# Moving two operands of one matrix product to other byte places in on-chip memory

## The chip, the cores and the metric

The kernel runs on one core of one Trainium2 chip. The metric is device time in microseconds (us) from the first to the last instruction of one execution. Three runs of the kernel before took 2555.57, 2558.36 and 2559.72 us; the median is 2558.36 us.

## What is computed

The reference is a spectral filter followed by a two-layer network, in single precision:

```
X  = rfft(x, axis=1)                       # x: 8 batches x 3008 positions x 256
Yr = X.real @ w_r - X.imag @ w_i + b_r     # the projection: 256 x 256 complex weights
Yi = X.real @ w_i + X.imag @ w_r + b_i
Yr, Yi = soft_threshold(Yr, 0.01), soft_threshold(Yi, 0.01)
y  = irfft(Yr + 1j * Yi, n=3008, axis=1)   # 24064 tokens x 256
h  = y @ w_in                              # first product:  256 -> 2048
g  = maximum(0.01 * h, h)
out = g @ w_out                            # second product: 2048 -> 256
```

## The kernel before

The length 3008 is split as 47 x 64, so the transforms are matrix products too. Each of the 8 batches passes three stages that go through DRAM: `fwd(b)` (sums of 47, constants `fa0` and `fa1`), `mid(b)` (sums of 64, projection, threshold, inverse sums of 64) and, for the tokens, `inverse` (the last sums of 47). Batches 0 and 1 of `fwd` and batch 0 of `mid` run ahead of the main loop in plain single precision. The main loop `moe()` takes tokens in 47 chunks of 512 and the 2048 hidden features in 8 steps `q` of 256 a chunk. A step issues the first product (`moe_a` and `moe_b`, a Strassen scheme of seven 256-column block products) and the second product (`moe_o`, 512 columns). Between the steps a `Stream` pulls a little of `fwd(b + 1)` and `mid(b)` of the next batch. The order on every engine is settled when the program is built; TensorE takes its matmuls strictly as they stand.

Wherever single precision is needed at the faster matmul rate, a value is held as two halves, high and low (type `F32R`), and a product is three matmuls: high x high, and the two mixed ones. A matmul has a *stationary* operand, which a weight load (LDWEIGHTS, row `PEld`) puts into the array, 128 columns wide, and a *moving* operand, which streams through it, 256 or 512 columns wide. Two helpers issue them: `products` (line 80) for everything but the network's first product, `block` (line 94) for that one.

The part that the change touches is `mid(b)` for batches 1 to 7, 12 steps `j` each:

- `stage_b(j)` multiplies by `fb` (line 358) and splits the result into the halves `eh` and `el`, slices of one tile `e2` of 128 x 2 x 2 x 3 x 128 values: ScalarE writes `eh` (lines 370, 373), VectorE `el` (lines 372, 374).
- `proj(j)` is the projection: three weights (`wr`, `wn`, `wd`) x two halves of the feature axis x three terms = 18 matmuls of 256 columns. The stationary operand is a 128-column slice of `e2`, the moving one a 256-column slice of a weight. In the profile these are line 80, `psf<-wr_hi,eh` and its like; `eh` stands there for the whole tile `e2`.

`pair` lays out the constants' halves: it asks for a tile with some spare room and uses it from element `skip` on, so that `skip` sets the byte place of the operand. `split_consts` calls it for the projection's weights (names that begin with w) and for the constants of the transforms.

The places where operands begin in the built program before, in bytes modulo 128 of a partition's address; every slice of an operand is a multiple of 128 bytes further on and so begins at the same place:

| matmuls | columns | count | moving | stationary |
|---|---|---|---|---|
| first product, line 94 (`yh`, `yl` x `win`) | 256 | 7728 | 64 | 0 |
| second product, line 622 (`gh`, `gl` x `wout`) | 512 | 4512 | 64 | 64 |
| projection, line 80 (`wr`, `wn`, `wd` x `eh`) | 256 | 1512 | 96 | 64 |
| inverse sums of 64, line 80 (`zh` x `gb`) | 512 | 252 | 64 | 64 |
| sums of 47, line 80 (`xz` x `fa`) | 512, 256 | 252 | 64 | 64 |

(The first chunk's 96 first products have 512 columns, at the same places as the others.)

Of the kernel before, what the change touches and what calls it, by code (L numbers as in the profile page):

```python
# [9 lines left out]
F32R = mybir.dt.float32r  # L10
# [10 lines left out]
P = 128  # L21
# [9 lines left out]
def spectral_mlp_kernel(  # L31
# [21 lines left out]
    NH = D // P  # L53
# [12 lines left out]
    sb = ctx.enter_context(tc.tile_pool(name="sb", bufs=2))  # L66
# [4 lines left out]
    def bank(tag, bufs):  # L71
        return ps.tile([P, 512], F32, name=tag, tag=tag, bufs=bufs)
# [29 lines left out]
    def pair(name, shape, skip, spare=0):  # L102

        n = 1
        for s in shape[1:]:
            n *= s
        room = -(-n // 32) * 32 + 32
        tiles = [
            const.tile([shape[0], room + k], F32R, name=f"{name}_{p}")[:, skip:skip + n]
            for p, k in (("hi", 0), ("lo", spare))  # L110
        ]
        if len(shape) == 4:
            tiles = [t.rearrange("p (a b c) -> p a b c", a=shape[1], b=shape[2]) for t in tiles]
        elif len(shape) == 3:
            tiles = [t.rearrange("p (a b) -> p a b", a=shape[1]) for t in tiles]
        consts[name] = tuple(tiles)
        return consts[name]

    def load_plain(name, src, shape):
        consts[name] = const.tile(shape, F32, name=name)  # L120
        sync.dma_start(consts[name], src)

    def split_consts():
        for name in ("wr", "wd", "wn", "gb", "fa0", "fa1"):
            w = consts[name + "32"][0]
            hi, lo = pair(name, list(w.shape), 16 if name[0] == "w" else 8, 32 if name == "gb" else 0)
            act.copy(hi, w)
            dve.tensor_sub(lo, w, hi.bitcast(F32))

# [197 lines left out]
    def mid(b):  # L327
# [21 lines left out]
        def stage_b(j):  # L349

            u = u_t.pop(j)
            pb = bank("psh", 4) if b < 1 else bank("psf", 2)
            pv = pb.rearrange("p (a c i k) -> p a c i k", a=NH, c=2, i=2)
            for i in range(2):
                k = 2 * j + i
                for dh in range(NH):
                    s = slice(dh * P, (dh + 1) * P)
                    nc.tensor.matmul(pv[:, dh, :, i, :], u[:, i, s], fbt[:, 0:k + 2:k + 1, :], start=True, stop=True)  # L358
            pv = pb.rearrange("p (a c m) -> p a c m", a=NH, c=2)
            if b == 0:  # L360
                ef = e0[:, j % 2]
                act.copy(ef[:, :, 0:2, :], pv)
                dve.tensor_add(ef[:, :, 2, :], ef[:, :, 0, :], ef[:, :, 1, :])
                e_t[j] = (ef,)
                return
            e2 = sb.tile([P, 2, NH, 3, P], F32R, name="eh", tag="e", bufs=1)
            eh, el = e2[:, 0], e2[:, 1]
            xi = sb.tile([P, NH, P], F32, name="xi", tag="xi", bufs=1)
            act.copy(xi, pv[:, :, 1, :])
            act.copy(eh[:, :, 0:2, :], pv)  # L370
            dve.tensor_add(xi, pv[:, :, 0, :], xi)
            dve.tensor_sub(el[:, :, 0:2, :], pv, eh[:, :, 0:2, :].bitcast(F32))
            act.copy(eh[:, :, 2, :], xi)
            dve.tensor_sub(el[:, :, 2, :], xi, eh[:, :, 2, :].bitcast(F32))
            e_t[j] = (eh, el)
# [62 lines left out]
        if b:  # L438
            for s in range(NPAIR):
                if s + 2 < NPAIR:  # L440
                    load(s + 2)
                with tc.issue_after(mlp[0].ins):
                    stage_b(s)
                yield 16 * P
                yield None
                yield from proj(s)
            stage_g(NPAIR - 1)
            yield 3 * CS
            return
        for s in range(NPAIR + 3):  # L450
            if s + 2 < NPAIR:
                load(s + 2)
            if s < NPAIR:
                stage_b(s)
                yield 16 * P
            if 0 <= s - 1 < NPAIR:
                yield from proj(s - 1)
            if 0 <= s - 3 < NPAIR:
                stage_g(s - 3)
                yield 3 * CS  # L460
# [246 lines left out]
    f0.to(0.01)  # L707
    load_win(0, (sync, act))
    load_plain("fb", fb, [P, NK1 + 1, N2])
    load_weights()  # L710
    sign = const.tile([P, NK1 + NPAIR], F32, name="sign")
# [10 lines left out]
    with tc.issue_after(turned[0].ins):  # L722
        split_consts()
# [8 lines left out]
    with tc.issue_after(reads[3].ins):  # L732
        load_plain("ga", ga, [PA, 2, P])
# [152 lines left out]
```

## Time and profile before

| | |
|---|---|
| median of three runs | 2558.36 us |
| the profiled execution | 2558.46 us, of which the span from first to last instruction is 2556.7 us |
| TensorE matmul (PE) | 2515.7 us busy, 98% of the span |
| weight loads (PEld) | 2259.0 us, 88% |
| VectorE (DVE) | 1881.0 us, 74% |
| ScalarE (ACT) | 1673.5 us, 65% |
| mean granted TensorE clock | 0.995 of full |

Matmuls are pipelined: the profile gives each a duration of 280 ns or so for 256 columns, but the next one starts long before it ends. What a matmul costs a busy TensorE is the distance from its start to the next start. The chain of work that ended last counts in this way (a piece of "x6" is six matmuls, and its time runs to the next piece), and so do the start times of the timeline.

### The profile page before, as it was taken

To read this page: it belongs to the slowest core of one execution; us is meant where nothing else is said; L and a number is where in the kernel's file an instruction comes from. 1 tells how busy PE (TensorE), PEld (TensorE's weight loads), DVE (VectorE), ACT (ScalarE), POOL (GpSimd) and SP (SyncE) were. 2 spreads that over 40 slices of the span, in tenths; PEclk is the share of its full clock that TensorE was granted. 3 is DMA by queue.
4 is the path that set the end of the run, shared out by engine and by line. 5 is a ranking of instruction groups with operands and counts; after the bars stand their busy time and mean duration, and the time that the engine had idled before them with its cause. 6 is when DMAs were issued, how large, how long until landed. Compare 5 with 4: busy or idle time off the path is not lost.

```text
span 2556.7 us, 42449 instructions
## 1 busy us (share of the span) xinstructions
PE 2515.7 (98%) x16204; PEld 2259.0 (88%) x16204; DVE 1881.0 (74%) x3460; ACT 1673.5 (65%) x3151; POOL 119.3 (5%) x96
## 2 busy tenths in 40 slices
PE   6999999999999999999999999999999999999999
PEld 4689888999899998999989999899998998999998
DVE  7787777777877778777787777876768777666675
ACT  4776666677666776667756676566665676656564
POOL 0001000000000000000000000000000000000000
PEclk8999999999999999999999999999999999999999
DMA  8631133111321113211142111411114111101000
GB/s 262 184 93 49 44 88 91 42 46 49 102 70 42 50 41 109 61 51 50 38 113 58 50 45 42 113 57 50 46 38 123 55 51 44 46 17 33 9 17 17
DMA packets 119904, 165.12 MB, mean 65 GB/s; under 512 B 13597, under 2 KB 69909, under 8 KB 119701
## 3 DMA queue, kind: packets, MB, share of 16 engines
q1 hardware_dynamic: 79112, 115.54, 14.9%
q10 hardware_dynamic: 40589, 46.87, 7.1%
q8 instruction: 128, 2.10, 0.3%
q14 instruction: 75, 0.61, 0.1%
HBM read 86.60 MB, written 75.76 MB: 64 GB/s over the span
## 4 chain that ended last, share of the span: by engine, by line
PE 90%; DMA 4%; DVE 3%; ACT 2%; issue 1%; SPq 1%; ACTq 0%; DVEq 0%
PE pso L622 38%; PE psh L94 34%; PE psf L80 11%; PE psf L495 3%; PE psf L358 3%; DMA xin<-x_dram 1%; PE psh L80 1%; DMA u<-u_dram 1%; DVE gl L575 1%; DMA u_dram<-xin 1%; DVE xz L270 0%; DMA v_dram<-v 0%; DVE gf L606 0%; ACT zf L413 0%; DMA vin<-v_dram 0%
## 5 line engine op out<-in xcount | busy, mean ns | idle before, releaser
L94 PE MATMUL psh<-yh,win_hi 128*128 128x256 f32 (+1 forms) x2608 | 737.2, 284 | 2.4 <-DVE gf L606 2.4
L94 PE MATMUL psh<-yl,win_hi 128*128 128x256 f32 (+1 forms) x2608 | 727.0, 279 | 0.0
L94 PE MATMUL psh<-yh,win_lo 128*128 128x256 f32 (+1 forms) x2608 | 726.5, 280 | 0.0
L575 DVE TENSOR_TENSOR gl<-gf,gh 128x1024 fp32r<-128x1024 f32 x376 | 461.1, 1226 | 309.7 <-ACT gh L573 300.5
L622 PE MATMUL pso<-gh,wout_hi 128*128 128x512 f32 x1504 | 592.3, 394 | 1.1 <-ACT gh L573 1.1
L622 PE MATMUL pso<-gh,wout_lo 128*128 128x512 f32 x1504 | 590.4, 393 | 0.0
L622 PE MATMUL pso<-gl,wout_hi 128*128 128x512 f32 x1504 | 588.7, 391 | 1.1 <-DVE gl L575 1.1
L94 PEld LDWEIGHTS psh<-yh,win_hi 128*128 128x128 f32 x2608 | 489.3, 188 | 19.9 <-DVE gf L606 4.9
L94 PEld LDWEIGHTS psh<-yl,win_hi 128*128 128x128 f32 x2608 | 490.5, 188 | 15.6 <-issue 0.5
L94 PEld LDWEIGHTS psh<-yh,win_lo 128*128 128x128 f32 x2608 | 489.1, 188 | 2.0
L573 ACT CAST gh<-gf 128x1024 fp32r<-128x1024 f32 x376 | 395.4, 1052 | 45.1 <-PE pso L622 35.3
L609 ACT ACTIVATE gf<-gf 128x768 f32<-128x768 f32 x368 | 311.8, 847 | 158.7 <-DVE gf L606 147.6
L622 PEld LDWEIGHTS pso<-gl,wout_hi 128*128 128x128 f32 x1504 | 282.6, 188 | 61.9 <-DVE gl L575 3.0
L622 PEld LDWEIGHTS pso<-gh,wout_hi 128*128 128x128 f32 x1504 | 282.7, 188 | 48.4 <-ACT gh L573 1.9
L622 PEld LDWEIGHTS pso<-gh,wout_lo 128*128 128x128 f32 x1504 | 282.6, 188 | 45.4 <-issue 0.2
L608 ACT ACTIVATE gf<-psh 128x256 f32<-128x256 f32 x368 | 141.6, 385 | 229.8 <-PE psh L94 223.4
L606 DVE TENSOR_TENSOR gf<-psh,u 128x512 f32<-128x512 f32 x368 | 252.7, 687 | 27.7 <-PE psh L94 25.3
L590 ACT COPY p<-psh 128x256 f32<-128x256 f32 x368 | 136.7, 371 | 153.3 <-PE psh L94 144.7
L395 POOL TENSOR_TENSOR kb<-bias,kc 128x512 f32<-128x512 f32 x84 | 116.7, 1389 | 2068.3 <-ACT kc L393 1865.4
L591 DVE TENSOR_TENSOR u<-psh,p 128x256 f32<-128x256 f32 x368 | 154.8, 421 | 71.8 <-ACT p L590 70.8
L593 DVE TENSOR_TENSOR gf<-psh,u 128x256 f32<-128x256 f32 x368 | 155.1, 422 | 30.4 <-PE psh L94 16.4
L594 DVE TENSOR_TENSOR gf<-psh,gf 128x256 f32<-128x256 f32 x368 | 154.8, 421 | 5.5
(128 smaller groups left out, 3179.4 us busy)
## 6 DMA issues: line engine op xcount, KB each, us to landing
u<-u_dram SPq DMA_DIRECT2D x192, 128.0 KB, 2.8
v_dram<-v ACTq DMA_DIRECT2D x192, 128.0 KB, 2.4
out_dram<-ob SPq DMA_DIRECT2D x94, 256.0 KB, 2.0
vin<-v_dram SPq DMA_DIRECT2D x96, 240.0 KB, 3.6
xin<-x_dram SPq DMA_DIRECT2D x90, 240.0 KB, 3.1
u_dram<-xin ACTq DMA_DIRECT2D x72, 240.0 KB, 2.4
u_dram<-xin SPq DMA_DIRECT2D x24, 240.0 KB, 4.3
raw<-w_out_dram SPq DMA_DIRECT2D x8, 512.0 KB, 4.9
```

The source lines that it names most:

```text
L80: last = nc.tensor.matmul(dst, a, b, start=(i == 0), stop=(i == len(terms) - 1))
L94: mlp[:] = [nc.tensor.matmul(dst, a, b, start=start and i == 0, stop=i == 2, skip_group_check=True)]
L573: cp = act.copy(gh, g)
L575: parted[:] = [cp, dve.tensor_sub(gl, g, gh.bitcast(F32))]
L590: act.copy(p1, b1[:, lo])
L591: dve.tensor_add(u2, b1[:, hi], p1)
L593: dve.tensor_add(g[:, 3], b2[:, hi], u2)
L594: dve.tensor_add(g[:, 3], b2[:, lo], g[:, 3])
L606: dve.tensor_add(g[:, 1:3], b2.rearrange("p (k n) -> p k n", k=2), u2.unsqueeze(1).broadcast_to([P, 2, HT]))
L608: act.activation(g[:, 0], b1[:, lo], AF.Prelu, alpha=SLOPE)
L609: act.activation(g[:, 1:4], g[:, 1:4], AF.Prelu, alpha=SLOPE)
L622: mlp[:] = [nc.tensor.matmul(po, a[:, f, s], r[:, i], start=(f == 0 and j == 0), stop=(f == NF - 1 and j == 2),)]
```

## The change

Two operands get other places. `split_consts` uses `skip` 8 in place of 16 for the projection's weights, 32 bytes earlier in tiles that stay where they were: they begin at 64 in place of 96 modulo 128. The tile `e2` comes from a new helper, `placed`, that asks for 32 more values a partition and gives out the part from value 16 on: it begins 64 bytes later, at 0 in place of 64 modulo 128. The projection then has the first product's places, moving 64 and stationary 0.

The tile `e2` is 6272 in place of 6144 bytes a partition, so every ring that lies behind it moves up by 128 bytes and keeps its place modulo 128: among them `z` (`zh`), `zf`, `u`, `v`, `wout_lo`, `kb`, `t`, `y`, `odd`, `p1` and `u2`. `win`, `yh`, `yl`, `wout_hi`, `gh` and `gl` stay where they were. No instruction is added, removed or moved: on every engine the same operations stand in the same order with the same waits, and only line numbers differ (9 more behind `placed`).

```diff
+    def placed(shape, name, tag, bufs):
+
+        n = 1
+        for k in shape[1:]:
+            n *= k
+        t = sb.tile([P, n + 32], F32R, name=name, tag=tag, bufs=bufs)[:shape[0], 16:16 + n]
+        axes = " ".join("abcd"[:len(shape) - 1])
+        return t.rearrange(f"p ({axes}) -> p {axes}", **dict(zip("abcd", shape[1:])))
+
...
     def split_consts():
         for name in ("wr", "wd", "wn", "gb", "fa0", "fa1"):
             w = consts[name + "32"][0]
-            hi, lo = pair(name, list(w.shape), 16 if name[0] == "w" else 8, 32 if name == "gb" else 0)
+            hi, lo = pair(name, list(w.shape), 8 if name[0] == "w" else 8, 32 if name == "gb" else 0)
...
-            e2 = sb.tile([P, 2, NH, 3, P], F32R, name="eh", tag="e", bufs=1)
+            e2 = placed([P, 2, NH, 3, P], "eh", "e", 1)
             eh, el = e2[:, 0], e2[:, 1]
```

## The prediction

> **What bounds the kernel now.** I read the page's engine totals first, then its chain by line, then the busy time by stage, and last the chain in order of time inside the stage that the change touches. The totals and the chain:
>
> ```profile
> PE 2515.7 (98%) x16204; PEld 2259.0 (88%) x16204; DVE 1881.0 (74%) x3460; ACT 1673.5 (65%) x3151; POOL 119.3 (5%) x96
> ...
> PE 90%; DMA 4%; DVE 3%; ACT 2%; issue 1%; SPq 1%; ACTq 0%; DVEq 0%
> PE pso L622 38%; PE psh L94 34%; PE psf L80 11%; PE psf L495 3%; PE psf L358 3%; DMA xin<-x_dram 1%; PE psh L80 1%; DMA u<-u_dram 1%; DVE gl L575 1%; DMA u_dram<-xin 1%; DVE xz L270 0%; DMA v_dram<-v 0%; DVE gf L606 0%; ACT zf L413 0%; DMA vin<-v_dram 0%
> ```
>
> TensorE has work in 98% of the span, and nine tenths of the chain that ended last run through its matmuls. The projection is part of "psf L80", 11% of the chain together with the inverse sums and the sums of 47. The three stages (start, main loop with `fwd` and `mid` between, main loop alone):
>
> ```profile
> 0.00:180.00 180.00, 151.24 (x640) 108.97 (x641) 137.79 (x237) 112.41 (x207) 2.05 (x7) 0.93 0.62 184
> 180.00:2190.00 2010.00, 2002.25 (x13233) 1822.84 (x13232) 1504.93 (x2803) 1347.51 (x2585) 117.23 (x89) 1.00 0.22 61
> 2190.00:2557.00 367.00, 362.21 (x2335) 327.17 (x2333) 238.24 (x421) 213.57 (x360) 0.00 (x0) 1.00 0.07 24
> ```
>
> The columns are the stretch, its length, then the busy time of PE, PEld, DVE, ACT and POOL. Between 180 and 2190 us PE is idle for 2010.00 - 2002.25 = 7.75 us, 0.4%. So a nanosecond less between two matmuls there is very nearly a nanosecond less of the whole, and nothing else sets the pace: DVE has 2010 - 1505 = 505 us to spare. All matmuls that the change touches lie in that stretch or within 5 us of its start, as the first and last starts of the projection's groups say:
>
> ```profile
> L80 PE MATMUL psf<-wr_hi,eh x336: 277/282/385, 175.5 to 2186.0; 128*128 128x256 f32 x168
> L80 PE MATMUL psf<-wn_hi,eh x336: 278/280/288, 175.7 to 2189.5; 128*128 128x256 f32 x168
> L80 PE MATMUL psf<-wd_hi,eh x336: 277/281/363, 176.4 to 2190.2; 128*128 128x256 f32 x168
> L80 PE MATMUL psf<-wr_lo,eh x168: 277/281/286, 175.6 to 2185.9; 128*128 128x256 f32 x168
> L80 PE MATMUL psf<-wn_lo,eh x168: 277/281/286, 175.8 to 2189.3; 128*128 128x256 f32 x168
> L80 PE MATMUL psf<-wd_lo,eh x168: 277/281/365, 176.6 to 2190.0; 128*128 128x256 f32 x168
> ```
>
> That is 3 x 336 + 3 x 168 = 1512 matmuls of 256 columns, 84 steps of 18. Their durations (median 281 ns) say nothing of their cost, since the next one starts long before; nor do those of the first product, which are as long:
>
> ```profile
> L94 PE MATMUL psh<-yl,win_hi 128*128 128x256 f32 x2576 | 714.4, 278 | 0.0
> L94 PE MATMUL psh<-yh,win_lo 128*128 128x256 f32 x2576 | 713.9, 278 | 0.0
> ```
>
> What a matmul costs is read from the chain in order of time, in a stretch without waits, where each piece ends as the next begins (start, us, what):
>
> ```profile
> 1686.74 2.75 PE pso L622 x12
> 1689.49 1.42 PE psf L80 x12
> 1690.90 2.43 PE psh L94 x21
> 1693.33 0.73 PE psf L80 x6
> 1694.06 2.76 PE pso L622 x12
> ```
>
> One whole step of the projection stands here: the x12 and the x6 of line 80 are its 18 matmuls. They take 1.42 + 0.73 = 2.15 us, 119.4 ns each. The first product's 21 between them, of the same width, in the same three-term scheme and with one weight load each, take 2.43 us, 115.7 ns each. Twenty microseconds on, a step is cut into smaller pieces:
>
> ```profile
> 1709.46 0.70 PE psh L94 x6
> 1710.16 0.72 PE psf L80 x6
> 1710.89 1.72 PE psh L94 x15
> 1712.60 0.72 PE psf L80 x6
> 1713.33 2.76 PE pso L622 x12
> ```
>
> Six of the first product take 116.7 ns each, six of the projection 120.0 ns, on both sides of fifteen of the first product at 114.7 ns. And late in the kernel, where no projection is left, a run of the first product goes at 2.40 / 21 = 114.3 ns:
>
> ```profile
> 2418.34 2.40 PE psh L94 x21
> 2420.74 2.74 PE pso L622 x12
> ```
>
> So the projection's matmuls are slower than the first product's in every piece where the two can be compared, by 3.3 to 5.3 ns. What differs between them by the program is the places (96 and 64 modulo 128 against 64 and 0), the PSUM bank they write and what stands before them; the shape, the term order and the one load for each matmul are alike.
>
> **The change part by part.** *The projection's two places.* After it the projection and the first product have the same two places, so I price the 1512 matmuls by the first product's rows. The trace doesn't hold a projection at these places; its price is bounded below by 114.3 ns (the long undisturbed run) and above by the present 119.4 ns. I take 115.7 ns, the run that stands right between two pieces of the projection, which is nearest in place and surroundings; a run of six alone would give 116.7. Gain: 1512 x (119.4 - 115.7) = 5.6 us. Of it 2002.25 / 2010.00 = 99.6% lies on a busy PE, which leaves 5.6; I take 5.5, since the shorter TensorE work now and then only meets a wait that was covered. The waits that could take it back are those of PE and its weight loads on VectorE and ScalarE, for which the groups show a few us in all:
>
> ```profile
> L94 PEld LDWEIGHTS psh<-yh,win_hi 128*128 128x128 f32 x2608 | 489.3, 188 | 19.9 <-DVE gf L606 4.9 <-issue 0.2 <-ACT yh L520 0.2
> L622 PE MATMUL pso<-gl,wout_hi 128*128 128x512 f32 x1504 | 588.7, 391 | 1.1 <-DVE gl L575 1.1
> ```
>
> With `gf` (line 606) and `gl` (line 575) late by 4.9 and 1.1 us over the whole kernel, they are next if PE gets ahead, but a step that is 0.07 us shorter out of some 24 us (2010 / 84) shortens what covers them by 0.3%.
>
> *The writes into the moved operands.* ScalarE and VectorE now write `eh` from place 0 in place of 64 (four instructions a step, lines 370 to 374), and the three weights once from 64 in place of 96. Writes of one shape, 128x512, to place 0 (`win`) and to place 64 (`zh`) stand in the trace:
>
> ```profile
> L421 DVE TENSOR_TENSOR zh<-zf,zh 128x512 fp32r<-128x512 f32 x84 | 57.7, 686 | 13.8 <-ACT zh L420 13.1
> L420 ACT CAST zh<-zf 128x512 fp32r<-128x512 f32 x84 | 51.9, 618 | 1.2
> L187 DVE TENSOR_TENSOR win_lo<-cva,win_hi 128x512 fp32r<-128x512 f32 x4 | 2.8, 688 | 1.3 <-ACT win_hi L186 1.3
> L186 ACT CAST win_hi<-cva 128x512 fp32r<-128x512 f32 x4 | 2.5, 619 | 8.4 <-DVE t L405 4.8 <-DVE cva L177 3.6
> ```
>
> 686 against 688 ns and 618 against 619 ns: 84 x 4 x 2 ns = 0.7 us at most, on two engines that have hundreds to spare. Cost zero; without that cover 0.7 us.
>
> *The rings that move by 128 bytes.* They keep their place modulo 128. If only that counts they cost nothing. If 256 counted, the second product's `wout_lo` would change class; the first product tells: its `win_hi` and `win_lo` start 128 bytes apart modulo 256 (at 128 and 0), and their rows above are 278 ns both. I take zero, and keep a loss as a rival.
>
> *The order, the DMA queues and SP.* No instruction moves on any engine, so no queue is passed and no wait added: zero.
>
> Sum, against the profiled execution's own 2558.46 us (span 2556.7 us and 1.8 us around it; it is within 0.1 us of the median 2558.36 us): 2558.46 - 5.5 = 2553.0 us, 0.21% less. A measurement of this kernel can tell about 0.2%, some 5.1 us, from no change, so the forecast lies just at that edge.
>
> **The rivals.** *The place is not the cause.* The 3 to 5 ns could come from what surrounds the projection: short pieces, and another class of matmul before each. The trace speaks partly for it: the first product's own price goes from 114.3 ns in a run of 21 to 116.7 ns in a run of six and to 115.7 ns behind a projection. Against it, like pieces still differ (six at 120.0 beside six at 116.7). Then nothing happens: 2558.5 us. [...]
>
> *More than the rows of its neighbours.* If a switch between places also slows the first product behind a projection (2.43 against 2.40 us for 21), about 0.03 us come back at each of one or two such switches a step: 84 to 168 x 0.03 = 2.5 to 5 us more. With the projection at 114.3 ns itself (1512 x 5.1 = 7.7 us) the end is 2558.46 - 7.7 - 2.5 = 2548.3 us. The undisturbed rows speak for it, but few are so clean.
>
> *Slower: `wout_lo` pays.* The second product's stationary `wout_lo` goes from 64 to 192 modulo 256. If the place modulo 256 decides the price there, and by as much as the best and worst places of 256 columns differ now (5.1 ns), 1504 matmuls lose 7.7 us:
>
> ```profile
> L622 PE MATMUL pso<-gh,wout_lo 128*128 128x512 f32 x1504 | 590.4, 393 | 0.0
> ```
>
> With the projection's gain that is 2558.46 - 5.5 + 7.7 = 2560.7 us, without it 2566.2 us. It ends slower than before from 5.5 us / 1504 = 3.7 ns a matmul on. Against it stands the equality of `win_hi` and `win_lo`.
>
> *The change does not do what it says.* The built program's places are those stated, so this has no chance of its own.
>
> **How the numbers follow.** The place is the cause and the projection goes at about the first product's price: 0.62, of which 0.44 come out over 5.1 us and 0.18 under. The larger gain with the switches is the upper tail of this and included. The place is not the cause: 0.27, all within 0.2%, but for 0.02 that some other effect of the move makes it faster. The `wout_lo` loss, or a like one on a moved ring: 0.11, of which 0.08 slower by over 0.2% and 0.03 within. Faster 0.46, same 0.46, slower 0.08. The predicted time is the likeliest case's, 2553.0 us, with a range of its own of 2549 to 2556. The range for 8 in 10 takes in no effect and the spread of the runs shown (1.4 us above the median), 2560.0, and below the larger gain, 2548.5.
>
> **What would show it.** In the profile after, a step of the projection (x12 and x6 of line 80 in the chain) should take 18 x 115.7 = 2.08 us in place of 2.15, and a run of six 0.70 in place of 0.72; the first product's and the second product's pieces should stay at 2.40 and 2.74. If the projection's pieces stay at 0.72 and 1.42, the place was not the cause. If pieces of the first product behind a projection fall to 2.40, the switch was. If "pso L622 x12" grows past 2.78, a moved ring has taken it back. The prediction is wrong beyond its range if the pair 64 and 0 has a price in the projection that no row of the first product shows.

## The result and the profile after

The changed kernel is slower: median 2563.51 us of 19 runs (2560.57 to 2567.85) against 2558.36 us of 19 runs of the kernel before (2554.06 to 2564.43). The ratio is 1.002, with a 95% interval of 1.0013 to 1.0027: 3 to 7 us lost where 5.5 us were forecast to be won, and beyond the range of 2548.5 to 2560.0.

The projection did get faster. The chain in order of time of the changed kernel, at the two places that were shown of the kernel before (start, us, what; line 631 is the second product's old line 622):

```profile
1691.30 1.41 PE psf L80 x12
1692.72 2.40 PE psh L94 x21
1695.12 0.70 PE psf L80 x6
1695.82 2.79 PE pso L631 x12
...
1711.31 0.72 PE psh L94 x6
1712.03 0.71 PE psf L80 x6
1712.74 1.72 PE psh L94 x15
1714.46 0.70 PE psf L80 x6
1715.16 2.79 PE pso L631 x12
```

A step of the projection, x12 and x6 of line 80, takes 1.41 + 0.70 = 2.11 us, where it took 2.15. The first product's 21 behind the projection take 2.40 where they took 2.43. But the second product's 12 take 2.79 where they took 2.75 and 2.76. The same stands late in the kernel, where there is no projection any more:

```profile
2418.93 2.40 PE psh L94 x21
2421.33 2.78 PE pso L631 x12
```

Before, that piece took 2.74. So what the second product loses does not come from a projection beside it, and the kernel has 4512 / 12 = 376 such pieces' worth of it. The groups say it too, with durations of 395 in place of 391 and 393 ns:

```profile
L631 PE MATMUL pso<-gl,wout_hi 128*128 128x512 f32 x1504 | 593.4, 395 | 1.1 <-DVE gl L584 1.1
L631 PE MATMUL pso<-gh,wout_lo 128*128 128x512 f32 x1504 | 593.5, 395 | 0.0
```

No wait has grown: behind the second bar stands the idle time ahead of them, 1.1 and 0.0 us as before, and in the main stretch TensorE is busy for the same share of the time, 2002.36 of 2010 us where it was 2002.25, with fewer matmuls done in it (13191 where it was 13233):

```profile
180.00:2190.00 2010.00, 2002.36 (x13191) 1817.76 (x13190) 1502.11 (x2796) 1347.01 (x2579) 115.61 (x88) 1.00 0.22 61
```

For the whole kernel I took the distance from each matmul's start to the next one's, by class, leaving out those that hold a wait (over 145 ns for 256 columns, over 270 ns for 512). Each class keeps at least 98% of its matmuls. Means in ns:

| | first product, 256 columns | projection, 256 | second product, 512 |
|---|---|---|---|
| before | 115.2 | 119.5 | 229.6 |
| after | 115.2 | 117.3 | 231.8 |
| difference x count | 0 | -2.2 x 1512 = -3.3 us | +2.3 x 4512 = +10.2 us |

Together +6.9 us; the span of the profiled executions went from 2556.7 to 2563.4 us, +6.7 us. By class that is the whole account. The first product's 0 hides two shifts, though: its 1541 matmuls in runs right behind a projection went from 115.7 to 114.7 ns (-1.4 us), and most of the others, behind the second product and other classes, from 115.0 to 115.3 ns (+1.9 us).

### The profile page after: what moved, and what is told of

The parts are those of the page before. It is cut to its first block, busy times and chain, and to the rows that moved or that the text cites. A ratio compares the mean times of both kernels' runs of the same rounds, so it can differ in the third digit from the quotient of the medians.

```text
span 2563.4 us, 42449 instructions
## 1 busy us (share of the span) xinstructions
PE 2522.5 (98%) x16204; PEld 2258.9 (88%) x16204; DVE 1882.9 (73%) x3460; ACT 1676.7 (65%) x3151; POOL 119.0 (5%) x96
## 4 chain that ended last, share of the span: by engine, by line
PE 90%; DMA 4%; DVE 2%; ACT 2%; issue 1%; SPq 0%; ACTq 0%; DVEq 0%
PE pso L631 38%; PE psh L94 34%; PE psf L80 11%; PE psf L504 3%; PE psf L367 3%; DMA xin<-x_dram 2%; PE psh L80 1%; DMA u_dram<-xin 1%; DMA u<-u_dram 1%; DVE gl L584 1%; DMA v_dram<-v 0%; DVE xz L279 0%; DVE gf L615 0%; ACT gh L582 0%; ACT zf L422 0%
```

## The experiments

In all twelve kernels the operations on every engine, their order and their waits are those of the kernel before; only places differ. Theory A: a ring that moved by 128 bytes slows the second product, by its place modulo 256. Rival B: the projection's new places disturb what follows it.

**The shift alone.** The kernel before, with the tile longer and the operands where they were:

```diff
-            e2 = sb.tile([P, 2, NH, 3, P], F32R, name="eh", tag="e", bufs=1)
+            e2 = sb.tile([P, 2 * NH * 3 * P + 32], F32R, name="eh", tag="e", bufs=1)[:, :2 * NH * 3 * P].rearrange(
+                "p (a b c d) -> p a b c d", a=2, b=NH, c=3)
```

> Edit to the kernel before: the tile of the projection's operand is 128 bytes longer at its end, and both operands of the projection stay where they were (96 and 64). So every ring behind it moves up by 128 bytes as in the changed kernel, and nothing else differs. Theory A (a moved ring slows the second product): its pieces of 12 take 2.78 us as in the changed kernel, against 2.74 before; the projection stays at 1.42 and 0.73; 4512 x 2.3 ns = 10 us on top, 2568 us. Rival B (the projection's new places slow what follows it): pieces stay at 2.74 and the time at 2558 us.

Measured: 2569.96 us, ratio 1.0049 (1.0036 to 1.0061). The chain of this kernel, in the stage of the projection (line 623 is the second product):

```profile
1692.34 2.78 PE pso L623 x12
1695.11 1.42 PE psf L80 x12
1696.53 2.43 PE psh L94 x21
1698.96 0.72 PE psf L80 x6
```

The projection is as slow as ever and the second product as slow as in the changed kernel (231.9 ns). Theory A holds, B falls: 128 bytes of unused room behind one tile cost 9 to 16 us.

**The places alone.** The changed kernel, with the rings behind moved by 256 in place of 128 bytes:

```diff
-        t = sb.tile([P, n + 32], F32R, name=name, tag=tag, bufs=bufs)[:shape[0], 16:16 + n]
+        t = sb.tile([P, n + 64], F32R, name=name, tag=tag, bufs=bufs)[:shape[0], 16:16 + n]
```

> Edit to the changed kernel: the helper asks for 64 more values, not 32, so that the rings behind the tile lie 256 bytes above their old places, not 128; the projection has its new places. Theory A with place modulo 256 as what counts: the second product is back at 2.74 a piece of 12, the projection keeps 1.41 and 0.70, and the time is 3 us under the kernel before, 2555 us. If any move of the rings hurts (not modulo 256): 2.78 and 2563 us or more. Rival B: 2.78 and 2563.5 us.

Measured: 2551.68 us, ratio 0.9977 (0.9968 to 0.9986). Its chain:

```profile
1706.05 0.70 PE psf L80 x6
1706.75 1.71 PE psh L94 x15
1708.45 0.70 PE psf L80 x6
1709.16 2.74 PE pso L631 x12
```

Both are fast. So what the change set out to do is worth some 6 us (the kernel before took 2557.91 us in the runs beside it), more than the 3 us expected from the projection's own matmuls: by the distances, the projection gives 3.4 us, the first product 0.27 ns x 7728 = 2.1 us (in the runs right behind a projection it goes from 115.7 to 114.6 ns) and the second product 0.35 ns x 4512 = 1.6 us.

**Which ring.** Two kernels on the changed one; in both the tile of `wout_lo` is 128 bytes longer, so the rings behind it are 256 bytes up. In the first `wout_lo` begins 128 bytes into it, in the second at its start:

```diff
-            sb.tile([P, NF, D], F32R, name=f"wout_{p}", tag=f"wout_{p}", bufs=1) for p in ("hi", "lo"))
+            sb.tile([P, NF * D + (32 if p == "lo" else 0)], F32R, name=f"wout_{p}", tag=f"wout_{p}", bufs=1)[
+                :, 32 if p == "lo" else 0:][:, :NF * D].rearrange("p (a b) -> p a b", a=NF) for p in ("hi", "lo"))
```

(the second kernel has 0 in place of the 32 that stands behind the comma.)

> Edit to the changed kernel: wout_lo alone begins 128 bytes later in a tile that is 128 bytes longer, so it lies at 64 modulo 256 again; z, zf and u stay 128 bytes up, the rings behind wout_lo (t, v, y, odd, p1, u2) are 256 up. A1 (the second product's own operand): pieces of 12 back at 2.74, about 2555 us. A2 (z, zf or u): still 2.78, 2563.5 us. A3 (the rings behind wout_lo, read and written by ScalarE and VectorE): 2.74 and 2555 us as A1; the next run parts these two.

> As the run before (the longer tile, rings behind wout_lo 256 bytes up), but wout_lo begins at the tile's start and stays at 192 modulo 256. A1: 2.78 a piece and 2563.5 us, as the changed kernel. A3: 2.74 and 2555 us.

Measured: 2552.63 us, ratio 0.9985 (0.9975 to 0.9994), with `wout_lo` back at 64 modulo 256, and 2565.07 us, ratio 1.0031 (1.0019 to 1.0042), with it at 192. The first kernel's chain and then the second's (line 632 is the second product in both):

```profile
1687.12 0.70 PE psf L80 x6
1687.82 2.75 PE pso L632 x12
```

```profile
1695.26 0.70 PE psf L80 x6
1695.96 2.78 PE pso L632 x12
```

These two differ by the start of `wout_lo` and nothing else. So the ring is `wout_lo`; `z`, `zf`, `u`, and all that ScalarE and VectorE keep behind it, are out.

**What about its place.** `wout_lo` is the stationary operand of only one in three of the second product's matmuls, and all three kinds slowed: by 2.6 ns (`wout_hi` with `gh`), 1.7 (`wout_lo`) and 2.5 (`wout_hi` with `gl`). Built on the places-alone kernel, both tiles 256 bytes longer, one kernel moves both halves by 128 bytes, the other only the high one:

```diff
+            sb.tile([P, NF * D + 64], F32R, name=f"wout_{p}", tag=f"wout_{p}", bufs=1)[
+                :, at:][:, :NF * D].rearrange("p (a b) -> p a b", a=NF) for p, at in (("hi", 32), ("lo", 32)))
```

(the other kernel has `("lo", 0)`.)

> Built on the places-alone kernel (2551.7 us). Both wout tiles are 256 bytes longer and both halves begin 128 bytes later in them: wout_hi and wout_lo at 192 modulo 256, gh and gl at 64 as ever, every other ring where it was modulo 256. R1 (what hurts is that the two stationary halves lie 128 bytes apart modulo 256): pieces of 12 stay at 2.74, about 2552 us. R2 (what hurts is a stationary operand at 192 beside a moving one at 64): all three terms are hit where one of three was, so 2.78 or more, 2562 us or more.

> The same longer tiles, but only wout_hi begins 128 bytes later: wout_hi at 192, wout_lo at 64 modulo 256. R1: 2.78 a piece and about 2562 us, as when wout_lo alone is at 192. R2: two of three terms are hit, so worse than one: over 2.78, more than 2562 us.

Measured: 2569.67 us, ratio 1.0050 (1.0036 to 1.0063), for both, and 2566.83 us, ratio 1.0040 (1.0026 to 1.0054), for the high half alone. One row of each, in that order:

```profile
2411.68 2.79 PE pso L632 x12
```

```profile
2412.28 2.79 PE pso L632 x12
```

R1, that the two halves must lie alike, falls: both at 192 are as bad. R2 holds in its sign and not in its size: 232.3 ns with one or both moved, so one stationary half at 192 beside a moving operand at 64 is enough to slow the whole stream. Not all of the loss lies in the second product: in these two kernels the first product goes at 115.7 and 115.5 ns, where it takes 115.0 in the places-alone kernel (0.7 and 0.5 ns x 7728, 5.7 and 4.1 us), although its own operands kept their places modulo 256. Modulo 512 `yh` and `yl` lie 256 bytes apart in these two kernels alone; whether that or the slow second product beside it is the cause is not shown.

Then distance or place? The kernel before, with all rings behind the constants moved up by 128 bytes:

```diff
-        consts[name] = const.tile(shape, F32, name=name)
+        if name == "ga":
+            consts[name] = const.tile([PA, 2 * P + 32], F32, name=name)[:, :2 * P].rearrange("p (a b) -> p a b", a=2)
+        else:
+            consts[name] = const.tile(shape, F32, name=name)
```

> Edit to the kernel before: the tile of the constant ga is 128 bytes longer, so every ring behind the constants moves up by 128 bytes together: gh, gl, wout_hi and wout_lo all lie at 192 modulo 256, where they were all at 64; yh and yl go to 192 beside win at 128 and 0; the constants stay. Rule D (the distance between moving and stationary modulo 256 decides): the second product stays at 2.74 a piece of 12, and the time at about 2558 us. Rule P (a stationary operand at 192 is slow by itself): 2.78 and 2568 us, as with the shift of the rear rings alone.

Measured: 2561.10 us, ratio 1.0013 (1.0004 to 1.0022). Late in this kernel (line 625 is the second product):

```profile
2410.92 2.39 PE psh L94 x21
2413.31 2.75 PE pso L625 x12
2416.05 2.39 PE psh L94 x21
2418.44 2.74 PE pso L625 x12
```

With everything at 192 the second product is fast again (229.8 ns): rule P falls, and rule D, that the distance between moving and stationary operand modulo 256 decides, holds for the two distances tried, 0 and 128. The expected 2558 us were missed by 3: in the stage of the projection the first product's runs behind it grew,

```profile
1690.40 1.42 PE psf L80 x12
1691.82 2.49 PE psh L94 x21
1694.31 0.71 PE psf L80 x6
```

from 2.43 to 2.49 us for 21, and its mean distance from 115.2 to 115.6 ns: 0.4 x 7728 = 3.1 us. In this kernel `yh` and `yl` are at 192, and it is the one kernel in which they moved modulo 256. That this is the cause is not shown: the first product took as long, 115.7 ns, in the kernel with both `wout` halves at 192, where `yh` and `yl` were at 64. The projection got a little faster, from 119.5 to 118.6 ns, with its stationary operand at 192 too.

**What the projection wants.** Its weights alone, in the kernel before (no ring moves):

```diff
-            hi, lo = pair(name, list(w.shape), 16 if name[0] == "w" else 8, 32 if name == "gb" else 0)
+            hi, lo = pair(name, list(w.shape), 8 if name[0] == "w" else 8, 32 if name == "gb" else 0)
```

> Edit to the kernel before: only the projection's weights begin 32 bytes earlier (moving 64, stationary still 64 modulo 128); no tile grows, so no ring moves. If the moving operand's place made the projection's gain, its pieces are 1.41 and 0.70 and the time is about 2555 us; if the stationary one's, they stay at 1.42 and 0.73 and 2558 us. The second product stays at 2.74 either way.

Measured: 2553.28 us, ratio 0.9986 (0.9977 to 0.9995). Its projection is at 118.0 ns, between 119.5 before and 117.2 with both places: the weights bring about two thirds of the projection's gain. The time fell by more than the projection's 1.5 ns x 1512 = 2.3 us, since the first product goes at 114.9 in place of 115.2 ns here too.

In the trace no projection had come down to the first product's 115 ns. Its weights' tiles are 2176 bytes long, an odd number of 128, so with the high halves at 64 modulo 256 the low ones lie at 192. Three kernels make both halves lie alike, with six tiles longer by 128 bytes:

```diff
-        room = -(-n // 32) * 32 + 32
+        room = -(-n // 32) * 32 + (64 if name in ("wr", "wd", "wn") else 32)
```

on the places-alone kernel (both at 64, stationary at 128 modulo 256), on the weights-alone kernel (both at 64, stationary at 64) and on the kernel before (both at 96, stationary at 64):

> Built on the places-alone kernel. The six tiles of the projection's weights are 128 bytes longer each, so high and low halves both begin at 64 modulo 256; so far the high ones are at 64 and the low ones at 192. All rings behind move by 768 bytes, a multiple of 256. If a gap of 128 between two halves that alternate slows the projection as it slowed the second product, its matmuls fall from 117.2 to about 114.5 ns each: 1512 x 2.7 = 4 us, 2548 us; pieces of 12 and 6 at 1.37 and 0.69. If the gap of moving halves doesn't matter: 1.41, 0.70 and 2552 us.

> Built on the weights-alone kernel (2553.3 us, moving 64 and 192, stationary 64 modulo 256): the six weight tiles are 128 bytes longer, so both halves lie at 64; the stationary operand stays at 64. If alike halves are what the projection needs and the stationary place is free: 115.3 ns a matmul as with the stationary at 128, pieces of 12 and 6 at 1.37 and 0.68, 2549 us. If the stationary place at 0 modulo 128 is needed too: 117 ns and 2552 us.

> Edit to the kernel before: only the longer weight tiles, so both halves begin at 96 modulo 256 (so far 96 and 224), the stationary operand stays at 64. If alike halves are all that counts: 115.3 ns a matmul, 2552 us. If 96 itself is a bad place: still 118 to 119.5 ns, 1.42 and 0.72 a piece, 2557 us.

Measured: 2548.25 us, ratio 0.9968 (0.9958 to 0.9979); 2552.40 us, ratio 0.9983 (0.9974 to 0.9992); 2555.81 us, ratio 0.9991 (0.9982 to 1.0001), the last not told apart from the kernel before. The chain of the first of them:

```profile
1697.43 2.72 PE pso L631 x12
1700.15 0.70 PE psh L94 x6
1700.86 0.68 PE psf L80 x6
1701.54 1.70 PE psh L94 x15
1703.23 0.68 PE psf L80 x6
```

Now six of the projection take 0.68 us where they took 0.72. The second of the three has its stationary operand at the same place as the moving one and is no better than the kernel before in the projection's own pieces:

```profile
1683.73 1.43 PE psf L80 x12
1685.16 2.40 PE psh L94 x21
1687.56 0.72 PE psf L80 x6
```

By the projection's mean distance the kernels stand like this:

| moving (high, low), stationary, modulo 256 | ns | kernel |
|---|---|---|
| 96, 224; 64 | 119.5 | before |
| 96, 224; 192 | 118.6 | all rings up by 128 |
| 64, 192; 64 | 118.0 | weights alone |
| 64, 192; 128 | 117.2 | places alone (117.3 in the changed kernel) |
| 64, 64; 64 | 119.1 | halves alike, stationary 64 |
| 96, 96; 64 | 118.1 | halves alike, moving 96 |
| 64, 64; 128 | 115.3 | halves alike, both places new (115.5 in the next kernel) |

With the moving halves at 64, alike halves help beside a stationary operand at 128 (117.2 to 115.3) and hurt beside one at 64 (118.0 to 119.1); neither of my two alternatives for that kernel had this. With the moving halves at 96, they help beside a stationary operand at 64 as well (119.5 to 118.1). So the second product's rule does not carry over: beside a stationary operand at 64, moving the low half from a distance of 128 to one of 0 made the projection slower. The kernel with all the projection's operands at 64 is under the kernel before all the same, by 5.6 us; the first product at 114.9 in place of 115.2 ns gives 0.34 x 7728 = 2.6 us of that, the projection and the second product some 1.1 us together, and the rest is not accounted for.

**The other constants.** Built on the best kernel, all halves of `gb` and `fa` at 64 beside `zh` and `xz` at 64:

```diff
-            for p, k in (("hi", 0), ("lo", spare))
+            for p, k in (("hi", spare), ("lo", 0))
...
-            const.tile([shape[0], room + k], F32R, name=f"{name}_{p}")[:, skip:skip + n]
+            const.tile([shape[0], room + k], F32R, name=f"{name}_{p}")[
+                :, skip + (32 if name[:2] == "fa" and p == "hi" else 0):][:, :n]
```

> Built on the kernel with alike halves (2548.3 us): the spare 128 bytes of gb go from its low half to its high one, and the high halves of fa begin 128 bytes later in their tiles, so all halves of gb and fa lie at 64 modulo 256, beside zh and xz at 64; so far gb_lo and the high halves of fa were at 192. Rule D: their 252 + 252 matmuls of mostly 512 columns lose some 3 to 4 ns each, up to 1.9 us together: 2546.5 us. If short runs never reach the fast rhythm: 2548 us.

Measured: 2548.95 us, ratio 0.9964 (0.9951 to 0.9976), so not told apart from 2548.25. The mean distance of the `gb` matmuls is 231.9 after 232.2, that of the 512-column `fa` ones 233.6 after 233.5. Nothing was won. They stand mostly in runs of one to three, and in the long runs of the second product, too, the first few matmuls are slow where the operands lie well (in the kernel before the first two of a run of 12 take 232 and 234 ns, the last six 227). That fits the second alternative; no run here tests it further.

## Why the prediction was wrong

- *The step that failed* is "The rings that move by 128 bytes", taken as zero. It is worth +10.2 us: 4512 matmuls, 2.3 ns each. The shift alone shows it (2569.96 us), and the pair of kernels that differ by the start of `wout_lo` names the ring.
- *Its argument* was that `win_hi` and `win_lo`, 128 bytes apart modulo 256, have equal rows. The rows compared were durations, which the same text had just called no measure of cost. And `win` could not show it: 128 and 0 both lie 64 away from the moving 64. What hurts in the second product is a distance of 128 (231.8 to 232.3 ns where 229.2 to 229.8 were measured without it), and no class of long runs in the trace before had one.
- *The rival "Slower: `wout_lo` pays"* is what happened, at the place named, given 0.11 with its like. Its size was misjudged on both sides: a price of 5.1 ns on 1504 matmuls was set down, and 2.3 ns on all 4512 came out, since the stream as a whole slows and not only the term whose operand moved. Its condition of 3.7 ns on 1504 would be 1.2 ns on 4512.
- *The projection's term*, 3.7 ns x 1512 = 5.6 us, was too high: 2.2 ns, 3.3 us. The price of 115.7 ns was taken from the first product at "the same two places" modulo 128, but modulo 256 the projection's two weight halves lay at different places, and the first product's moving operands do not. With alike halves at 64, beside a stationary operand at 128, the projection does go at 115.3 ns, and six take 0.68 us, under the 0.70 forecast.
- *"More than the rows of its neighbours"* has its effect: with the places alone, the first product speeds up, mostly behind the projection (2.1 us in all). That a switch between places causes it is not shown: with the weights alone moved, where the stationary operands still differ (64 against 0 modulo 128), the runs behind a projection go at 114.6 ns too. That the 2551.7 us of the places-alone kernel lie near the 2553.0 forecast is luck: the projection's term was too large by 2.2 us, and the gains of its neighbours, which the sum left out, made up for it.
- *"The place is not the cause"* fell: kernels that differ in nothing but places have medians from 2548 to 2570 us, and the projection's matmuls of 256 columns went from 119.5 to 115.3 ns between places that are all multiples of 32 bytes.
- *The writes, the order and the waits* were priced rightly at zero: the operations and waits are the same, and TensorE's busy share in the main stretch is 2002.4 of 2010 us.

What stays open is why. Distance 128 modulo 256 is slow in the 512-column second product (231.8 to 232.3 ns) and distance 0 fast (229.2 to 229.8 ns); in the 256-column projection 64 with alike halves is the best of those tried (115.3 ns) and 0 hardly better than the old places (119.1 against 119.5 ns). No run here shows the cause of either, nor why the first product slowed beside a slow second product; moving `gh` and `gl` apart from `wout` was not tried.

## What to carry to other kernels

A change of one tile's size is a change of place for every tile allocated behind it. Before costing it, list the places of all operands of the busiest engine before and after, modulo 256 and not only modulo the number that the change speaks of; here padding to a multiple of 256 turned a loss of 5 us into a gain of 6, and padding the weights' halves alike made it 9 (2548.25 us, ratio 0.9968). And price a matmul by the distance to the next start, in comparisons too: the first product's rows show durations of 278 to 282 ns, and its matmuls start 115.2 ns apart on average. A comparison of places tells only about the distances that occur in it: `win_hi` and `win_lo` both lie 64 from their partner, so their equality said nothing of 128.

## What the runs showed of the hardware

In these kernels the places where a matmul's two operands begin in on-chip memory changed its pace. In the second product a matmul took 231.8 to 232.3 ns on average in the five kernels in which a stationary half lies 128 bytes modulo 256 from the moving operand, and 229.2 to 229.8 ns in the others, whether all lie at 64 or all at 192. The loss was not the misplaced operand's alone: with one operand in three misplaced all three kinds slowed by 1.7 to 2.6 ns, and moving the high half, alone or with it, made 232.3 of 231.8 ns. Before the change a run of 12 settled to 227 ns a matmul after five; with `wout_lo` misplaced the second to the eleventh matmul took 230 to 234 ns on average and only the last one 228. In those five kernels the first product slowed a little as well: late in the kernel (after 2195 us), where no projection is left, it takes 114.3 to 114.4 ns in the kernels whose second product is fast and whose `yh` and `yl` are at 64, and 114.5 to 115.9 ns in the five where a `wout` half is misplaced.
